# A spectral filter finished on VectorE with one inverse matmul per class: swapped rows by DMA instead of a second matmul

## The chip, the cores and the metric

The kernel runs on one core of a Trainium2 chip. The metric is the device time of one execution in microseconds (us); a comparison takes the median of several runs. The engines are TensorE (in the profile PE for matmuls and PEld for weight loads), VectorE (DVE), ScalarE (ACT), GpSimd (POOL) and SyncE (SP). The last two do little more here than issue DMA transfers: GpSimd the inputs and the output, SyncE the trips of intermediate results through DRAM.

## The reference

Two parts follow each other. A filter over the sequence (3008 positions, 8 batches, 256 channels) multiplies the real Fourier transform of x by a complex filter; then every token goes through a small network with a sine.

```python
X = np.fft.rfft(x, axis=1)                     # x: (8, 3008, 256)
Y = X * (filt_r + 1j * filt_i)[None, :, :]     # 1505 frequencies
y = np.fft.irfft(Y, n=3008, axis=1)
h = y.reshape(24064, 256) @ w_in               # w_in: (256, 2048)
s = np.sin(alpha * h)
out = (h + s * s / (alpha + 1e-09)) @ w_out    # w_out: (2048, 256)
```

## The kernel before

The transform of length 3008 = 47 x 64 is done as two short ones with twiddles folded into the second table. For each batch there are three stages of small pieces, with a trip through DRAM (a store and a transposed read) between them:

- stage 1, 8 pieces: transform of length 47 (`pa`), result `t1`, stored to `d1`, read back as `t2`;
- stage 2: transform of length 64 for two of the 24 classes a piece (`pb`, rows 0 to 63 the real and 64 to 127 the imaginary parts), product with the filter, inverse transform of length 64 (`pc`), result `g`, stored to `d2`;
- stage 3, 16 pieces: the inverse transform of length 47 (`pd`) from the reload `t4`, result `y`.

```python
def stage2(u):
    if u < 12:
        ps = (ops if b == 0 else fps).tile([128, 2, C], FP32, ...)          # pb
        for i in range(2):
            s = 2 * u + i
            nc.tensor.matmul(out=ps[:, i, :], lhsT=d_t[:, s, :], rhs=st["t2"][s // 6][:, s % 6, :], ...)
        xf = xfpool.tile([128, 2, C], FP16, ...)
        nc.scalar.copy(out=xf, in_=ps)
        pr = []
        for k in range(2):                            # times Re(F), times Im(F)
            pt = ppool.tile([128, 2, C], FP16, ...)
            nc.vector.tensor_tensor(out=pt, in0=xf, in1=f_t[k][:, 2 * u:2 * u + 2, :], op=ALU.mult)
            pr.append(pt)
        st["p", u] = pr
    if u > 0:
        w = u - 1
        pr = st.pop(("p", w))
        ...
        ps = fps.tile([128, 2, C], FP32, ...)                               # pc
        for i in range(2):
            for k in range(2):                        # two inverse tables, summed in PSUM
                nc.tensor.matmul(out=ps[:, i, :], lhsT=e_t[:, k, 2 * w + i, :], rhs=pr[k][:, i, :],
                                 start=(k == 0), stop=(k == 1))
        evac(st["g"][:, i0:i0 + 2, :], ps, ...)       # ScalarE or VectorE in turn
        if w % 3 == 2:
            ...                                       # two stores of g to d2, on SyncE
```

The second table `e_t[:, 1]` is the first one with its halves exchanged and one negated: it does the part of the complex product that mixes real and imaginary rows.

The network works on blocks of 512 tokens, eight steps a block. A step has four matmuls of 512 columns (`ph`, `hidden`), a sine on ScalarE and a square on VectorE, and nine matmuls of 256 columns for the block before (`po`, `project`). The pieces of the next batches are put between the steps by a plan, in which batch b's tokens begin at step 48b:

```python
plan = {1: [-45 + i for i in range(8)],
        2: [-29 + 14 * i / 13 for i in range(13)],
        3: [-10, -9] + [-7 + 2 * i for i in range(14)]}
...
at_step = 48 * b + plan[stage][at[stage]]
if b == 1 and stage == 1:
    at_step = 9 + at[stage]
```

Batch 0 has nothing to run beside. Its stages come first, and the load of `w_out` is told to wait for its first reload `t4`. A scheduler then orders the instructions of each engine, so a piece may stand a step or two behind the plan.

Of the kernel before, what the change touches and what calls it, by code (L numbers as in the profile page):

```python
# [9 lines left out]
FP16 = mybir.dt.float16  # L10
FP32 = mybir.dt.float32
# [43 lines left out]
def kernel(  # L55
# [33 lines left out]
    xpool = pool("xp", 4)  # L89
    t1pool = pool("t1", 4)  # L90
    t2pool = pool("t2", 4)
    xfpool = pool("xf", 3)
    ppool = pool("pp", 4)
    gpool = pool("gp", 4)
    t4pool = pool("t4", 3)
# [8 lines left out]
    wf_t = cpool.tile([NR, NK], FP16)  # L104
    nc.sync.dma_start(out=wf_t, in_=wf_dram.ap())
    d_t = cpool.tile([128, NS, 128], FP16)
    e_t = cpool.tile([128, 2, NS, 128], FP16)
    wi_t = cpool.tile([NK, NR], FP16)
    f_t = [cpool.tile([128, NS, C], FP16, name=f"filt{i}") for i in range(2)]

# [27 lines left out]
    def spectral(b):  # L138

        pieces = []  # L140
        d1 = dpool.tile([2 * NS, N2, C], FP16, name=f"d1_{b}", tag="d1")
        d2 = dpool.tile([2 * NS, N2, C], FP16, name=f"d2_{b}", tag="d2")
        d1_rows = d1.rearrange("a (h n) c -> (a h) n c", h=2)
        d2_rows = d2.rearrange("a (h n) c -> (a h) n c", h=2)
        st = {}

        def stage1(u):
            ch, half = divmod(u, 2)
            if u == 0:
                st["x"] = load_x(b)  # L150
            if half == 0:
                st["t1"] = t1pool.tile([NK, 8, C], FP16, name=f"t1_{b}_{ch}", tag="t1")
            for i in range(2):
                n0 = 4 * half + 2 * i
                ps = fps.tile([128, 512], FP32, name=f"pa_{b}_{u}_{i}", tag="f")
                marks["pe"] = nc.tensor.matmul(out=ps[0:NK, :], lhsT=wf_t, rhs=st["x"][ch][:, n0:n0 + 2, :],  # L156
                                               start=True, stop=True)
                evac(st["t1"][:, n0:n0 + 2, :], ps[0:NK, :])
            if half == 1:
                nc.sync.dma_start(out=d1_rows[:, 8 * ch:8 * ch + 8, :], in_=st["t1"])  # L160
            if u == 7:
                st["t2"] = []
                for g in range(4):
                    t2 = t2pool.tile([128, 6, C], FP16, name=f"t2_{b}_{g}", tag="t2")
                    for p in range(2):
                        a0 = p * NS + 6 * g
                        eng = nc.scalar if b == 0 and p else nc.sync
                        marks["t2", g] = eng.dma_start(out=t2[64 * p:64 * p + 64, :, :],
                                          in_=d1[a0:a0 + 6, :, :].rearrange("s n c -> n s c"))
                    st["t2"].append(t2)  # L170

        def stage2(u):
            if u < 12:

                ps = (ops if b == 0 else fps).tile([128, 2, C], FP32, name=f"pb_{b}_{u}",
                                                   tag="o" if b == 0 else "f")
                for i in range(2):
                    s = 2 * u + i
                    nc.tensor.matmul(out=ps[:, i, :], lhsT=d_t[:, s, :],  # L179
                                     rhs=st["t2"][s // 6][:, s % 6, :], start=True, stop=True)  # L180
                xf = xfpool.tile([128, 2, C], FP16, name=f"xf_{b}_{u}", tag="xf")
                nc.scalar.copy(out=xf, in_=ps)
                pr = []
                for k in range(2):
                    pt = ppool.tile([128, 2, C], FP16, name=f"p_{b}_{u}_{k}", tag="p")
                    marks["prod", u] = nc.vector.tensor_tensor(out=pt, in0=xf, in1=f_t[k][:, 2 * u:2 * u + 2, :],
                                                               op=ALU.mult)
                    pr.append(pt)
                st["p", u] = pr
            if u > 0:  # L190
                w = u - 1
                pr = st.pop(("p", w))
                if w % 3 == 0:
                    st["g"] = gpool.tile([128, 6, C], FP16, name=f"g_{b}_{w}", tag="g")
                ps = fps.tile([128, 2, C], FP32, name=f"pc_{b}_{w}", tag="f")
                for i in range(2):
                    for k in range(2):
                        nc.tensor.matmul(out=ps[:, i, :], lhsT=e_t[:, k, 2 * w + i, :],  # L198
                                         rhs=pr[k][:, i, :], start=(k == 0), stop=(k == 1))
                i0 = 2 * (w % 3)  # L200
                evac(st["g"][:, i0:i0 + 2, :], ps, i0 != 2 if b == 0 else None)
                if w % 3 == 2:
                    for p in range(2):
                        a0 = p * NS + 6 * (w // 3)
                        nc.sync.dma_start(out=d2[a0:a0 + 6, :, :].rearrange("s n c -> n s c"),
                                          in_=st["g"][64 * p:64 * p + 64, :, :])

        def stage3(u):
            ch, rest = divmod(u, 4)
            half, cb = divmod(rest, 2)  # L210
            if rest == 0:
                t4 = t4pool.tile([NK, 8, C], FP16, name=f"t4_{b}_{ch}", tag="t4")
                marks["t4"] = nc.sync.dma_start(out=t4, in_=d2_rows[:, 8 * ch:8 * ch + 8, :])
                st["t4"] = t4
            ps = fps.tile([128, 4, 128], FP32, name=f"pd_{b}_{u}", tag="f")
            psv = ps.rearrange("p a b -> p (a b)")[:, 0:4 * NR].rearrange("p (a r) -> p a r", r=NR)
            for i in range(4):
                nc.tensor.matmul(out=psv[:, i, :],
                                 lhsT=st["t4"][:, 4 * half + i, cb * 128:cb * 128 + 128],
                                 rhs=wi_t, start=True, stop=True)  # L220
            n0 = 8 * ch + 4 * half
            evac(y[:, cb, b % 2, n0:n0 + 4, :], psv)

        for u in range(8):
            pieces.append((1, lambda u=u: stage1(u)))
        for u in range(13):
            pieces.append((2, lambda u=u: stage2(u)))
        for u in range(16):
            pieces.append((3, lambda u=u: stage3(u)))
        return pieces  # L230
# [10 lines left out]
    first = spectral(0)  # L241
    for _, piece in first[:8]:
        piece()

# [19 lines left out]
    def dup_filter(g):  # L264
        gs = slice(6 * g, 6 * g + 6)
        for k in range(2):
            ins = nc.vector.tensor_copy(out=f_t[k][64:128, gs, :], in_=f_t[k][0:64, gs, :])
            behind(ins, marks["prod", 3 * g - 2] if g else s1_dve)

    for g in range(4):  # L270
        for k, filt in enumerate((filt_r, filt_i)):
# [8 lines left out]
    for g in range(3):  # L280
        pse = ops.tile([128, 8, 128], FP16, name=f"pse_{g}", tag="o")
        for i in range(8):
            behind(nc.tensor.transpose(out=pse[:, i, :], in_=d_t[:, 8 * g + i, :], identity=id16),
                   s1_pe)
        gs = slice(8 * g, 8 * g + 8)
        behind(nc.scalar.mul(e_t[:, 0, gs, :], pse, 0.125), s1_act)
        nc.vector.tensor_copy(out=e_t[0:64, 1, gs, :], in_=e_t[64:128, 0, gs, :])
        nc.vector.tensor_scalar(out=e_t[64:128, 1, gs, :], in0=e_t[0:64, 0, gs, :],
                                scalar1=-1.0, scalar2=None, op0=ALU.mult)

    ones = cpool.tile([128, 128], FP32)
    nc.vector.memset(ones, 1.0)
# [24 lines left out]
    w1T = cpool.tile([128, 16, C], FP16)  # L317
# [16 lines left out]
    def weights_out(i):  # L334
# [6 lines left out]
        if i < 4:  # L341
            pst = ops.tile([128, 8, 128], FP16, name=f"pst_{i}", tag="o")
            for cb in range(2):
                for t in range(4):
# [4 lines left out]
            for cb in range(2):  # L349
                nc.scalar.copy(out=w1T[:, 4 * i:4 * i + 4, cb * 128:cb * 128 + 128],  # L350
                               in_=pst[:, 4 * cb:4 * cb + 4, :])
        elif i >= 6:
            cb = i - 6
            psm = ops.tile([128, 2, C], FP32, name=f"psm_{cb}", tag="o")
            for jb in range(16):
                behind(nc.tensor.matmul(out=psm[:, 0, :], lhsT=w1T[:, jb, cb * 128:cb * 128 + 128],
                                        rhs=w2[:, jb, :], start=(jb == 0), stop=(jb == 15)),
                       marks["hidden"])
            nc.vector.tensor_copy(out=m_t[:, cb, :], in_=psm[:, 0, :])
# [44 lines left out]
    def store(o_blk, pb, col):  # L404

        p = 0
        while p < 128:
# [9 lines left out]

    plan = {1: [-45 + i for i in range(8)],
            2: [-29 + 14 * i / 13 for i in range(13)],
            3: [-10, -9] + [-7 + 2 * i for i in range(14)]}
    pending = [(1 + i % 4 + 8 * (i // 4), 0, piece) for i, (_, piece) in enumerate(first[25:])]
    for b in range(1, B):
        at = {1: 0, 2: 0, 3: 0}
        for stage, piece in spectral(b):
            at_step = 48 * b + plan[stage][at[stage]]
            if b == 1 and stage == 1:
                at_step = 9 + at[stage]  # L430
            at[stage] += 1
            pending.append((at_step, b, piece))
    pending.sort(key=lambda p: p[0])
    step = 0
# [44 lines left out]
```

## Time and profile before

| | before |
|---|---|
| median of 3 runs | 883.02 us (882.61 to 884.25) |
| span of the profiled run | 881.2 us |
| DMA moved | 94.99 MB, mean 108 GB/s |
| SyncE queue (hardware_dynamic q1) | 57008 packets, 50.36 MB, 22.0% of 16 engines |
| GpSimd queue (software_dynamic q0) | 23728 packets, 42.77 MB, 21.7% |
| HBM read, written | 58.02 MB, 49.81 MB |

Where the profile names a group, L198 are the inverse matmuls `pc`, L179 the forward ones `pb`, L186 the products on VectorE, L380 the squares, L375 and L390 the matmuls of the network. Tile numbers such as `t_2_0_2060` belong to one allocation; the first number is the batch. L160 stores `d1`, L168 reads `t2`, L205 stores `d2`, L213 reads `t4`. A timeline line has the start, the duration, engine, line, operation, tiles and how many instructions it merges; for a DMA the duration is that of its issue and not of the transfer. What an engine waited for stands in square brackets.

### The profile page before, as it was taken

The page shows a single profiled execution, that of the slowest core. Times are in us where ns is not written, and L with a number is a line of the kernel's source. Part 1 is how long each engine was busy: PE and PEld are TensorE (multiplying, and loading weights), DVE is VectorE, ACT ScalarE, POOL GpSimd, SP SyncE. Part 2 cuts the span into 40 slices and gives each one's busy share as a digit, 9 for nine tenths or more (in the row PEclk, how much of TensorE's full clock was granted, in tenths as well). Part 3 has the DMA queues.
Part 4 walks back from the last instruction along what each step waited for, and adds up shares of the span by engine and source line. Part 5 has one row for each costly group of instructions (what it writes and reads, how often), then busy time and mean ns, then how long its engine had stood idle before and what let it go on. Part 6 is the DMA issues. An engine that isn't in the chain of part 4 may idle for free.

```text
span 881.2 us, 15647 instructions
## 1 busy us (share of the span) xinstructions
PE 839.1 (95%) x6233; PEld 585.2 (66%) x6233; DVE 503.9 (57%) x886; ACT 521.1 (59%) x671; POOL 255.3 (29%) x495
## 2 busy tenths in 40 slices
PE   6759899999999999999999999999999999999993
PEld 2336677667776677767776677767776677667673
DVE  4737575566646565465756566565755666455441
ACT  4545565566656665666656666566656666555550
POOL 3211223333233232332233323233232232333332
PEclk9969999999999999999999999999999999999997
DMA  9984834185334724175343823256242533311111
GB/s 217 246 236 87 194 79 108 51 171 119 84 110 114 156 69 117 54 152 123 79 123 91 179 71 99 75 131 150 68 115 67 134 77 79 108 37 33 36 42 32
DMA packets 82737, 94.99 MB, mean 108 GB/s; under 512 B 12700, under 2 KB 64932, under 8 KB 82664
## 3 DMA queue, kind: packets, MB, share of 16 engines
q1 hardware_dynamic: 57008, 50.36, 22.0%
q0 software_dynamic: 23728, 42.77, 21.7%
q10 hardware_dynamic: 1928, 0.86, 0.5%
q8 instruction: 49, 0.80, 0.4%
q14 instruction: 24, 0.20, 0.1%
HBM read 58.02 MB, written 49.81 MB: 122 GB/s over the span
## 4 chain that ended last, share of the span: by engine, by line
PE 89%; DMA 6%; DVE 2%; issue 1%; ACT 0%; POOL 0%; SPq 0%; POOLq 0%; DVEq 0%
DMA w_out_502<-in_moe_w_out_dram 1%; DMA t_1_0_939<-d_1_504 1%; DMA d_7_517<-g_9_8756 1%; DMA d_0_107<-t_0_3_159 1%; DMA x_0_109<-in_x_dram 1%; DMA t_7_0_8931<-d_7_517 1%; DMA t_0_1_176<-d_0_107 0%; DMA t_0_0_476<-d_0_108 0%; PE po_0_5494 L390 0%; PE po_0_7950 L390 0%; PE po_2_4348 L390 0%; PE po_2_838 L390 0%; PE po_2_1892 L390 0%; PE po_0_705 L390 0%; PE po_0_4463 L390 0%
## 5 line engine op out<-in xcount | busy, mean ns | idle before, releaser
L375 PEld LDWEIGHTS <-w_465 128*128 128x128 f16 x1536 | 150.3, 98 | 100.4 <-issue 2.3
L198 PEld LDWEIGHTS <-e_t 128*128 128x128 f16 x384 | 37.5, 99 | 12.8 <-issue 2.5
L394 PEld LDWEIGHTS <-y 128*128 128x128 f16 x376 | 36.7, 98 | 4.7
L179 PEld LDWEIGHTS <-d_t 128*128 128x128 f16 x192 | 18.7, 100 | 27.6 <-DMA t_0_0_173<-d_0_107 3.5
L156 PEld LDWEIGHTS <-wf_t 94*96 94x96 f16 x128 | 16.5, 129 | 18.8 <-issue 9.4
L380 DVE TENSOR_TENSOR v_9644<-v_9644 128x1024 f16<-128x1024 f16 x8 | 5.5, 693 | 8.0 <-ACT v_9644 L379 8.0
L380 DVE TENSOR_TENSOR v_9789<-v_9789 128x1024 f16<-128x1024 f16 x8 | 5.5, 693 | 8.0 <-ACT v_9789 L379 8.0
L380 DVE TENSOR_TENSOR v_9488<-v_9488 128x1024 f16<-128x1024 f16 x8 | 5.5, 693 | 7.7 <-ACT v_9488 L379 7.7
L380 DVE TENSOR_TENSOR v_3898<-v_3898 128x1024 f16<-128x1024 f16 x8 | 5.5, 691 | 7.1 <-ACT v_3898 L379 7.1
L380 DVE TENSOR_TENSOR v_8810<-v_8810 128x1024 f16<-128x1024 f16 x8 | 5.5, 690 | 7.1 <-ACT v_8810 L379 7.1
L380 DVE TENSOR_TENSOR v_2681<-v_2681 128x1024 f16<-128x1024 f16 x8 | 5.5, 690 | 7.1 <-ACT v_2681 L379 7.1
L380 DVE TENSOR_TENSOR v_7593<-v_7593 128x1024 f16<-128x1024 f16 x8 | 5.5, 690 | 7.1 <-ACT v_7593 L379 7.1
L380 DVE TENSOR_TENSOR v_6354<-v_6354 128x1024 f16<-128x1024 f16 x8 | 5.5, 690 | 7.1 <-ACT v_6354 L379 7.1
L380 DVE TENSOR_TENSOR v_1442<-v_1442 128x1024 f16<-128x1024 f16 x8 | 5.5, 690 | 7.1 <-ACT v_1442 L379 7.1
L380 DVE TENSOR_TENSOR v_5137<-v_5137 128x1024 f16<-128x1024 f16 x8 | 5.5, 690 | 7.1 <-ACT v_5137 L379 7.1
L380 DVE TENSOR_TENSOR v_1608<-v_1608 128x1024 f16<-128x1024 f16 x8 | 5.5, 693 | 7.1 <-ACT v_1608 L379 7.1
L380 DVE TENSOR_TENSOR v_6520<-v_6520 128x1024 f16<-128x1024 f16 x8 | 5.5, 693 | 7.1 <-ACT v_6520 L379 7.1
L380 DVE TENSOR_TENSOR v_8976<-v_8976 128x1024 f16<-128x1024 f16 x8 | 5.5, 692 | 7.1 <-ACT v_8976 L379 7.1
L380 DVE TENSOR_TENSOR v_9147<-v_9147 128x1024 f16<-128x1024 f16 x8 | 5.5, 692 | 7.1 <-ACT v_9147 L379 7.1
L380 DVE TENSOR_TENSOR v_9317<-v_9317 128x1024 f16<-128x1024 f16 x8 | 5.5, 692 | 7.1 <-ACT v_9317 L379 7.1
L380 DVE TENSOR_TENSOR v_4064<-v_4064 128x1024 f16<-128x1024 f16 x8 | 5.5, 692 | 7.1 <-ACT v_4064 L379 7.1
L274 POOL DMA_DIRECT2D filt_101<-in_filt_r_dram x8 | 4.6, 587 | 16.9 <-DMA t_0_0_173<-d_0_107 15.0
(2527 smaller groups left out, 2688.4 us busy)
## 6 DMA issues: line engine op xcount, KB each, us to landing
w_in_469<-in_moe_w_in_dram POOLq DMA_DIRECT2D x2, 1024.0 KB, 9.2
w_out_502<-in_moe_w_out_dram POOLq DMA_DIRECT2D x1, 2048.0 KB, 12.3
filt_101<-in_filt_r_dram POOLq DMA_DIRECT2D x8, 96.0 KB, 7.0
filt_102<-in_filt_i_dram POOLq DMA_DIRECT2D x8, 96.0 KB, 7.4
d_t<-d_tbl SPq DMA_DIRECT2D x1, 768.0 KB, 7.9
d_0_107<-t_0_0_117 SPq DMA_DIRECT2D x1, 384.0 KB
d_0_107<-t_0_1_131 SPq DMA_DIRECT2D x1, 384.0 KB, 6.5
d_0_107<-t_0_2_145 SPq DMA_DIRECT2D x1, 384.0 KB
```

Source lines behind the costliest of these rows:

```text
L156: marks["pe"] = nc.tensor.matmul(out=ps[0:NK, :], lhsT=wf_t, rhs=st["x"][ch][:, n0:n0 + 2, :], start=True, stop=True)
L179: nc.tensor.matmul(out=ps[:, i, :], lhsT=d_t[:, s, :], rhs=st["t2"][s // 6][:, s % 6, :], start=True, stop=True)
L198: nc.tensor.matmul(out=ps[:, i, :], lhsT=e_t[:, k, 2 * w + i, :], rhs=pr[k][:, i, :], start=(k == 0), stop=(k == 1))
L274: ins = nc.gpsimd.dma_start(out=f_t[k][32 * q:32 * q + 32, 6 * g:6 * g + 6, :], in_=bass.AP(tensor=filt.tensor, offset=filt.offset + off, ...
L375: marks["hidden"] = nc.tensor.matmul(out=ps[:, i, 0:n], lhsT=w1[:, cb, jb * 128:jb * 128 + 128], rhs=y_cols[:, cb, c0:c0 + n], start=(cb = ...
L380: marks["square"] = nc.vector.tensor_tensor(out=vs, in0=vs, in1=vs, op=ALU.mult)
L394: nc.tensor.matmul(out=dst, lhsT=y_cols[:, cb, c0 + 128 * t:c0 + 128 * t + 128], rhs=m_t[:, cb, :], start=False, stop=(cb == 1))
```

## The change

The mixing part of the complex product moves from a second inverse matmul to VectorE. A copy `xs` of the spectrum with real and imaginary rows exchanged is made; VectorE forms xf times Re(F), xs times plus or minus Im(F), and their sum, and one inverse matmul per class follows. For batch 0 the exchanged spectrum is computed by TensorE itself (four half-width matmuls a piece and one more copy on ScalarE). For the other batches two DMAs on the SyncE queue copy it from SBUF to SBUF, for groups of three pieces, and the inverse comes five pieces behind the forward transform instead of one. The filter's imaginary part gets its sign by a negation of half its rows. To make room, `w1T` takes its space from the pool of `g`. The plan of pieces differs too: the diff replaces the one above.

```diff
-    xfpool = pool("xf", 3)
+    xfpool = pool("xf", 6)
...
-    e_t = cpool.tile([128, 2, NS, 128], FP16)
+    e_t = cpool.tile([128, NS, 128], FP16)
...
+        def forward(u):
+            ...                                   # tiles xf and xs for three pieces
+            nc.scalar.copy(out=xf[:, i0:i0 + 2, :], in_=ps)
+            if b == 0:
+                ps = ops.tile([128, 2, C], FP32, name=f"pw_{b}_{u}", tag="o")
+                for i in range(2):
+                    s = 2 * u + i
+                    for h in range(2):
+                        nc.tensor.matmul(out=ps[64 * h:64 * h + 64, i, :],
+                                         lhsT=d_t[:, s, 64 - 64 * h:128 - 64 * h],
+                                         rhs=st["t2"][s // 6][:, s % 6, :], start=True, stop=True)
+                nc.scalar.copy(out=xs[:, i0:i0 + 2, :], in_=ps)
+            elif u % 3 == 2:
+                for h in range(2):
+                    nc.sync.dma_start(out=xs[64 * h:64 * h + 64], in_=xf[64 - 64 * h:128 - 64 * h])
+
+        def inverse(w):
+            i0 = 2 * (w % 3)
+            pr = []
+            for k, name in enumerate(("xf", "xs")):
+                pr.append(ppool.tile([128, 2, C], FP16, name=f"p_{b}_{w}_{k}", tag="p"))
+                marks["prod", w] = nc.vector.tensor_tensor(
+                    out=pr[k], in0=st[name, w // 3][:, i0:i0 + 2, :],
+                    in1=f_t[k][:, 2 * w:2 * w + 2, :], op=ALU.mult)
+            nc.vector.tensor_tensor(out=pr[0], in0=pr[0], in1=pr[1], op=ALU.add)
+            ...
+            for i in range(2):
+                nc.tensor.matmul(out=ps[:, i, :], lhsT=e_t[:, 2 * w + i, :], rhs=pr[0][:, i, :],
+                                 start=True, stop=True)
+            evac(st["g"][:, i0:i0 + 2, :], ps)
+            ...                                   # stores to d2 as before
+
+        lag = 1 if b == 0 else 5
...
+            if k == 1:
+                nc.vector.tensor_scalar(out=f_t[1][0:64, gs, :], in0=f_t[1][0:64, gs, :],
+                                        scalar1=-1.0, scalar2=None, op0=ALU.mult)
...
-        behind(nc.scalar.mul(e_t[:, 0, gs, :], pse, 0.125), s1_act)
-        nc.vector.tensor_copy(out=e_t[0:64, 1, gs, :], in_=e_t[64:128, 0, gs, :])
-        nc.vector.tensor_scalar(out=e_t[64:128, 1, gs, :], in0=e_t[0:64, 0, gs, :],
-                                scalar1=-1.0, scalar2=None, op0=ALU.mult)
+        behind(nc.scalar.mul(e_t[:, gs, :], pse, 0.125), s1_act)
...
-    plan = {1: [-45 + i for i in range(8)],
-            2: [-29 + 14 * i / 13 for i in range(13)],
-            3: [-10, -9] + [-7 + 2 * i for i in range(14)]}
+    starts = {1: -36, 2: -23, 3: -5}
+    steps = {1: 8, 2: 16, 3: 16}
+    count = {1: 8, 2: 17, 3: 16}
...
-            at_step = 48 * b + plan[stage][at[stage]]
+            i = at[stage]
+            at[stage] += 1
+            at_step = 48 * b - 8 + starts[stage] + i * steps[stage] / count[stage]
             if b == 1 and stage == 1:
-                at_step = 9 + at[stage]
+                at_step = 9 + i
```

More of the change, by code (lines that the diff above doesn't have):

```diff
@@ L170, in stage1 @@
                     st["t2"].append(t2)
+        def forward(u):
+            if u % 3 == 0:
+                for name in ("xf", "xs"):
+                    st[name, u // 3] = xfpool.tile([128, 6, C], FP16, name=f"{name}_{b}_{u}",
+                                                   tag="xf")
+            i0 = 2 * (u % 3)
+            xf, xs = st["xf", u // 3], st["xs", u // 3]
+            ps = (ops if b == 0 else fps).tile([128, 2, C], FP32, name=f"pb_{b}_{u}",
+                                               tag="o" if b == 0 else "f")
+            for i in range(2):
+                s = 2 * u + i
+                nc.tensor.matmul(out=ps[:, i, :], lhsT=d_t[:, s, :],
+                                 rhs=st["t2"][s // 6][:, s % 6, :], start=True, stop=True)
[3 more added lines that the diff above has]
+                for i in range(2):
+                    s = 2 * u + i
+                    for h in range(2):
+                        nc.tensor.matmul(out=ps[64 * h:64 * h + 64, i, :],
+                                         lhsT=d_t[:, s, 64 - 64 * h:128 - 64 * h],
+                                         rhs=st["t2"][s // 6][:, s % 6, :], start=True, stop=True)
+                nc.scalar.copy(out=xs[:, i0:i0 + 2, :], in_=ps)
+            elif u % 3 == 2:
+                for h in range(2):
+                    nc.sync.dma_start(out=xs[64 * h:64 * h + 64], in_=xf[64 - 64 * h:128 - 64 * h])
@@ new lines, in inverse @@
+        def inverse(w):
[7 more added lines that the diff above has]
+            nc.vector.tensor_tensor(out=pr[0], in0=pr[0], in1=pr[1], op=ALU.add)
+            if w % 3 == 0:
+                st["g"] = gpool.tile([128, 6, C], FP16, name=f"g_{b}_{w}", tag="g")
+            ps = fps.tile([128, 2, C], FP32, name=f"pc_{b}_{w}", tag="f")
+            for i in range(2):
+                nc.tensor.matmul(out=ps[:, i, :], lhsT=e_t[:, 2 * w + i, :], rhs=pr[0][:, i, :],
+                                 start=True, stop=True)
+            evac(st["g"][:, i0:i0 + 2, :], ps)
+            if w % 3 == 2:
+                for p in range(2):
+                    a0 = p * NS + 6 * (w // 3)
+                    nc.sync.dma_start(out=d2[a0:a0 + 6, :, :].rearrange("s n c -> n s c"),
+                                      in_=st["g"][64 * p:64 * p + 64, :, :])
@@ L172, in stage2 @@
+        lag = 1 if b == 0 else 5
         def stage2(u):
             if u < 12:
[L175 to L206, printed above, removed]
@@ L208, in stage3 @@
+                forward(u)
+            if u >= lag:
+                inverse(u - lag)
         def stage3(u):
@@ L225, in spectral @@
             pieces.append((1, lambda u=u: stage1(u)))
-        for u in range(13):
+        for u in range(12 + lag):
             pieces.append((2, lambda u=u: stage2(u)))
@@ L267, in dup_filter @@
             ins = nc.vector.tensor_copy(out=f_t[k][64:128, gs, :], in_=f_t[k][0:64, gs, :])
-            behind(ins, marks["prod", 3 * g - 2] if g else s1_dve)
+            behind(ins, marks["prod", 3 * g - 3] if g else s1_dve)
+            if k == 1:
+                nc.vector.tensor_scalar(out=f_t[1][0:64, gs, :], in0=f_t[1][0:64, gs, :],
+                                        scalar1=-1.0, scalar2=None, op0=ALU.mult)
     for g in range(4):
@@ L316 @@
     m_t = cpool.tile([128, 2, C], FP16)
-    w1T = cpool.tile([128, 16, C], FP16)
+    w1T = [gpool.tile([128, 6, C], FP16, name=f"w1T_{i}", tag="g") for i in range(3)]
     w_in32 = vpool.tile([128, 2, DFF], FP32, name="w_in32", tag="v")
@@ L348, in weights_out @@
                                                identity=id16), marks["hidden"])
-            for cb in range(2):
-                nc.scalar.copy(out=w1T[:, 4 * i:4 * i + 4, cb * 128:cb * 128 + 128],
-                               in_=pst[:, 4 * cb:4 * cb + 4, :])
+            for h in range(2):
+                j0 = 4 * i + 2 * h
+                nc.scalar.copy(
+                    out=w1T[j0 // 6][:, j0 % 6:j0 % 6 + 2, :].rearrange("p j (a c) -> p a j c", a=2),
+                    in_=pst.rearrange("p (a j) c -> p a j c", a=2)[:, :, 2 * h:2 * h + 2, :])
         elif i >= 6:
@@ L355, in weights_out @@
             for jb in range(16):
-                behind(nc.tensor.matmul(out=psm[:, 0, :], lhsT=w1T[:, jb, cb * 128:cb * 128 + 128],
+                behind(nc.tensor.matmul(out=psm[:, 0, :], lhsT=w1T[jb // 6][:, jb % 6, cb * 128:cb * 128 + 128],
                                         rhs=w2[:, jb, :], start=(jb == 0), stop=(jb == 15)),
@@ L427 @@
         for stage, piece in spectral(b):
-            at_step = 48 * b + plan[stage][at[stage]]
+            i = at[stage]
+            at[stage] += 1
+            at_step = 48 * b - 8 + starts[stage] + i * steps[stage] / count[stage]
             if b == 1 and stage == 1:
-                at_step = 9 + at[stage]
-            at[stage] += 1
+                at_step = 9 + i
             pending.append((at_step, b, piece))
```

## The prediction

> **What bounds the kernel now.** I read the busy shares first, then the busy time by stretches, then the chain that ended last. The page begins:
>
> ```profile
> span 881.2 us, 15647 instructions
> PE 839.1 (95%) x6233; PEld 585.2 (66%) x6233; DVE 503.9 (57%) x886; ACT 521.1 (59%) x671; POOL 255.3 (29%) x495
> ```
>
> PE looks full, but matmul ends overlap, so I checked stretches (columns: window, length, then busy us of PE, PEld, DVE, ACT, POOL with counts, granted clock, DMA share, GB/s):
>
> ```profile
> 27.00:44.00 17.00, 13.00 (x72) 7.25 (x70) 15.51 (x36) 11.00 (x20) 6.09 (x10) 0.92 1.10 272
> 44.00:51.50 7.50, 0.00 (x0) 0.00 (x0) 3.23 (x3) 0.00 (x0) 0.00 (x0) 0.50 0.72 192
> 245.00:490.00 245.00, 245.00 (x1862) 173.09 (x1861) 146.43 (x253) 153.71 (x199) 75.30 (x146) 1.00 0.46 111
> ```
>
> Two regimes. From about 105 us on PE never idles: I took the start-to-start times of consecutive matmuls, and they are the streaming times, 216 ns for 512 columns, 109 for 256, 41 for 94, with no gap. There a removed matmul is saved time. At 27 to 44 us (middle stage of batch 0) VectorE is the full engine, 15.5 of 17 us; then PE waits 7.5 us for a round trip through DRAM.
>
> The later batches need two such trips each, both hidden by the distance between pieces. Batch 2, first trip: its last stage-1 matmul ends at 188.2 and the transposed read `t2` goes out when the stores have landed:
>
> ```profile
> 189.32 0.30 SPq L160 DMA_DIRECT2D d_2_506<-t_2_3_2030  x1
> 197.29 1.28 SPq L168 DMA_DIRECT2D t_2_0_2060<-d_2_506  x2
> ```
>
> It lands at 201.5 (3.5 us after the second issue) and is used at 205.5: 13.3 us needed, 17.3 available. Second trip: the last inverse matmul ends at 237.7, then
>
> ```profile
> 238.52 1.25 SPq L205 DMA_DIRECT2D d_2_507<-g_9_2627  x2
> 243.78 0.31 SPq L213 DMA_DIRECT2D t_2_0_2801<-d_2_507  x1
> ```
>
> By the DMA records this read lands at 246.8 and is used at 248.6: 9.1 needed, 10.9 available. In batch 7 that trip already shows as a stall:
>
> ```profile
> 753.99 0.34 PE L218 MATMUL pd_0_8933<-wi_t,t_7_0_8931 96*128 96x94 f16 x4 [0.29 <-DMA t_7_0_8931<-d_7_517]
> ```
>
> **What the Trainium skill says.** "TensorE: Matmul & The Clock Gate", section "Back-to-back issue gap", gives N/2.4 + 2.5 ns for a warm matmul, 109 ns at 256 columns; the trace agrees (109). "DMA: Bandwidth & Descriptors", section "Anatomy of one DMA", puts about 2 us of fixed cost on a DMA, mostly the receipt of the write. The quietest stores here take 2.9 us to land, so a swap by DMA costs latency, hardly bandwidth. "VectorE: DVE Perf Modes", section "The perf-mode tier table", caps a tensor_tensor at 2x, while a plain copy from SBUF may go 4x: the added sum will cost as much as a product. The trace has 418 ns for a 128x512 product, 335 ns from start to start when packed.
>
> **The change part by part.**
>
> 1. Inverse matmuls: 24 of 256 columns fewer per batch. Batches 1 to 7: 7 x 24 x 109 ns = 18.3 us, all on the path. Gain 18.3.
>
> 2. Batch 0 fits the VectorE-bound stage. Before, its stage is 24 products (8.0 us), 6 copies of the filter (3.1), 4 evacuations (2.4) = 13.6 us. After, by the built program's order: 36 products and sums x 0.335 = 12.1, 6 copies 3.1, 3 negations at about 0.43 = 1.3, 6 evacuations x 0.608 = 3.6, and some 0.8 for sums that wait for their own product = 20.9 us. The last evacuation is on VectorE too, just behind its matmul. Net about 6.3 us later. PE gets 48 half-width matmuls, ScalarE 12 more copies (30 x 0.48 = 14.4 us); both stay below VectorE. What follows (store, reload, the 12.3 us load of w_out that waits for this reload) is serial, so the 6.3 us go through to the end. Loss 6.3.
>
> 3. The schedule, which the short description does not name, is the largest item. Stage 1 now runs at steps 48b-44 to -37 and stage 2 starts at -31; before, -45 to -38 and -29: two or three steps less of distance. Stage 2 is longer (17 pieces at lag 5) and ends at -15; stage 3 starts at -13 instead of -10. I counted the matmuls in the built order of the new program and gave each its streaming time. A plain step (4 x 216 + 9 x 109 ns) is 1.85 us.
> First trip: 10.9 us available (17.3 before). Needed, from before, in batches 2 to 6: 13.3, 12.7, 12.8, 12.7, 12.8; in batch 7, with no x of a next batch loading beside it, 9.9. Stalls 2.4 + 1.8 + 1.9 + 1.8 + 1.9 + 0 = 9.8; the x loads stand in the same places, so I keep 9.4 after rounding down for noise. Batch 1 keeps its distance and its present 3.4 us stall.
> Second trip: 7.6 us available (10.9 before), as the order holds stage 3 back to about 4 steps behind the last inverse. Needed: 8.6 to 10.5 in the seven batches (issue of the reload 5.5 to 6.9 us after the last inverse, plus about 3.1 of reload). Stalls 1.0 to 2.9. The stores should be a little less disturbed, as the neighbouring output stores move by a step: 1.3 each, 9. Loss 18.4 together.
>
> 4. The swap. Per group of three pieces: two DMAs of 192 KB on the SyncE queue. From the last forward matmul: ScalarE's copy ends 1.3 us later (behind a 1.02 us sine), issue 0.65, landing about 2.9 like the quiet stores, then a product, a neighbour's product and the sum, 1.2: about 6.2 us with semaphores. The order leaves 6.4, 6.7, 7.6 and 6.3. Hidden, but barely; I allow 0.4 us a batch.
>
> 5. VectorE in stage 2. In twelve steps it now has 36 products and sums (12.1), 12 squares x 0.609 (7.3), 6 evacuations (3.6), 3 output copies (2.0) and 1.2 of own waits: 26.2 us; PE has 7 x 2.28 + 5 x 2.07 = 26.3. That is full, and it runs in order, with PE waiting for its sums and its evacuations. I allow 0.6 us a batch. Parts 4 and 5: 7.
>
> Sum: 883 - 18.3 + 6.3 + 18.4 + 7 = 896; I say 895.
>
> **The rivals.** (a) Plain PE saving: if the trips and the swap stay hidden and start-up does not move, 883 - 18 = 865. For it: 140 us and 245 us stretches with PE at 100%. Against: the distances in 3 are below what the trace shows as needed in six and seven batches. (b) VectorE takes over: if swap and sums stall each group of three by 1 us, 28 groups add 28 instead of 7, about 916. For it: 26.2 against 26.3 us. Against: squares have slack of more than a step, and idle time outside stage 2 is ample (57% busy overall). (c) Start-up hides its 6 us, because the DMA for w_out or the filters ends it anyway: 889. Against: w_out is issued only behind the reload. (d) The trips get shorter since stage 1 no longer runs beside stage 3 of the batch before: half the stalls vanish, 886.
>
> **Range and chances.** The saving is certain to 1 us; start-up to 3, the trips to 6, swap and VectorE to 8, combined about 10 to 11: 880 to 910 for 8 in 10. Faster by 2% needs under 865.4, which is rival (a) whole: 0.05. Slower by 2% needs over 900.7, five above the centre: 0.28. Within: 0.67.
>
> **What would show it.** PE has 6233 matmuls less 192 plus 48 = about 6089. PE waits of 1.5 to 2.5 us on the `t2` read at the head of stage 2 in batches 2 to 6 and not in 7, and of 1 to 3 us on the `t4` read at the head of stage 3 in every batch. The first reload of batch 0 is issued at about 54 us instead of 47.6. VectorE's busy time rises by 96 x 0.42 = 40 us, to about 540. Waits for `xs` on VectorE are short. If the two trips do not show on PE, part 3 fails and the time is near 878; if PE waits for sums in most groups, rival (b) holds.

## The result and the profile after

| | before | after |
|---|---|---|
| median | 882.82 us (882.27 to 884.25, 4 runs) | 894.67 us (892.17 to 896.36, 4 runs) |
| ratio | | 1.0129, 95% interval 1.0099 to 1.016 |
| span of the profiled run | 881.2 us | 894.1 us |
| SyncE queue | 57008 packets, 50.36 MB, 22.0% | 61488 packets, 61.38 MB, 26.0% |

The change costs 12 us, which is within 2%. The page of the changed kernel begins:

```profile
span 894.1 us, 15435 instructions
PE 834.7 (93%) x6089; PEld 565.5 (63%) x6089; DVE 531.3 (59%) x982; ACT 529.1 (59%) x681; POOL 254.9 (29%) x495
```

The count of matmuls is the predicted 6089. VectorE is busy 27 us more, not 40: packed operations of 0.42 us start 0.335 us apart, and busy time counts their overlap once. Products and sums count 33.8 us more, the squares 4.4 less, as more of them now overlap with a neighbour. The stretches, with the columns of before:

```profile
27.00:44.00 17.00, 15.06 (x85) 6.23 (x86) 14.00 (x32) 14.20 (x26) 5.65 (x10) 1.00 1.01 243
44.00:52.00 8.00, 3.34 (x12) 0.76 (x12) 7.20 (x20) 2.27 (x5) 0.00 (x0) 0.58 0.42 95
52.00:61.00 9.00, 0.76 (x8) 0.68 (x9) 5.17 (x5) 0.23 (x1) 0.25 (x1) 0.50 0.60 153
245.00:490.00 245.00, 238.72 (x1818) 165.74 (x1816) 151.24 (x279) 151.16 (x194) 72.74 (x141) 1.00 0.48 118
```

Two things are to be seen. Batch 0's middle stage now fills the stretch up to 52 us, and the hole that follows it (the trip through DRAM) lies there instead of at 44 us. And in the long steady stretch PE, which never paused before, is idle for 6.3 of 245 us.

The two trips of batch 2 by the timeline: first the last store of stage 1, the transposed read and the matmul that waits for it, then the store of stage 2, the reload and its matmul.

```profile
203.39 0.30 SPq L160 DMA_DIRECT2D d_2_562<-t_2_3_2126  x1
209.62 1.28 SPq L168 DMA_DIRECT2D t_2_0_2156<-d_2_562  x2
213.92 0.39 PE L184 MATMUL pb_0_2283<-t_2_0_2156,d_t 128*128 128x256 f16 x2 [0.57 <-DMA t_2_0_2156<-d_2_562]
...
251.04 1.25 SPq L220 DMA_DIRECT2D d_2_563<-g_9_2688  x2
254.79 0.31 SPq L236 DMA_DIRECT2D t_2_0_2786<-d_2_563  x1
258.34 0.34 PE L241 MATMUL pd_0_2788<-wi_t,t_2_0_2786 96*128 96x94 f16 x4 [0.38 <-DMA t_2_0_2786<-d_2_563]
```

Both reads, which used to land before they were wanted, are now waited for. Batch 0's reload and its first use show the later start; the first two lines are from before:

```profile
47.62 0.32 SPq L213 DMA_DIRECT2D t_0_0_476<-d_0_108  x1
51.51 0.49 PE L218 MATMUL pd_0_478<-wi_t,t_0_0_476 96*128 96x94 f16 x4 [8.68 <-DMA t_0_0_476<-d_0_108]
...
56.46 0.32 SPq L236 DMA_DIRECT2D t_0_0_532<-d_0_108  x1
...
60.24 0.49 PE L241 MATMUL pd_0_534<-wi_t,t_0_0_532 96*128 96x94 f16 x4 [8.33 <-DMA t_0_0_532<-d_0_108]
```

For the whole run I took the start-to-start time of consecutive matmuls, subtracted the streaming time of the first, and booked the rest on the matmul that came late. From the first stage-3 matmul of batch 0 on:

| PE time lost ahead of, us | before | after | after by batch 1 to 7 |
|---|---|---|---|
| first `pb` of batches 1 to 7 (first trip) | 3.3 | 8.7 | 3.3, 0.7, 1.9, 1.0, 1.8, 0, 0 |
| first `pd` of batches 1 to 7 (second trip) | 0.5 | 6.7 | 1.2, 0.6, 1.2, 0.8, 0.8, 1.3, 0.8 |
| `pc` of batches 1 to 7 (sum on VectorE) | 1.4 | 10.9 | 2.2, 1.2, 2.4, 1.4, 1.3, 1.2, 1.2 |
| everything else | 10.8 | 12.1 | |
| sum | 16.0 | 38.4 | |

The balance closes: 22.4 us more lost here, 8.7 us later in starting, 18.3 us of matmuls less, together 12.8; the spans differ by 12.9.

### The profile page after: what moved, and what is told of

The parts are those of the page before. It is cut to its first block, busy times and chain, and to the rows that moved or that the text cites. A ratio compares the mean times of both kernels' runs of the same rounds, so it can differ in the third digit from the quotient of the medians.

```text
span 894.1 us, 15435 instructions
## 1 busy us (share of the span) xinstructions
PE 834.7 (93%) x6089; PEld 565.5 (63%) x6089; DVE 531.3 (59%) x982; ACT 529.1 (59%) x681; POOL 254.9 (29%) x495
## 3 DMA queue, kind: packets, MB, share of 16 engines
q1 hardware_dynamic: 61488, 61.38, 26.0%
## 4 chain that ended last, share of the span: by engine, by line
PE 71%; DMA 16%; DVE 5%; ACT 3%; issue 2%; SPq 1%; POOL 0%; DVEq 0%; POOLq 0%; ACTq 0%
DMA w_out_558<-in_moe_w_out_dram 1%; DMA d_3_564<-t_3_3_3336 1%; DMA d_4_566<-t_4_3_4566 1%; DMA d_2_562<-t_2_3_2126 1%; DMA t_1_0_995<-d_1_560 1%; SPq L220 1%; DMA t_5_0_5806<-d_5_568 1%; DMA d_5_568<-t_5_3_5776 1%; DMA d_0_107<-t_0_3_159 1%; DMA x_0_109<-in_x_dram 1%; DMA xs_9_3739<-xf_9_3738 1%; DMA xs_9_1299<-xf_9_1298 1%; DMA t_0_0_173<-d_0_107 0%; DMA t_3_0_3995<-d_3_565 0%; ACT v_980 L405 0%
## 5 line engine op out<-in xcount | busy, mean ns | idle before, releaser
L214 PEld LDWEIGHTS <-e_t 128*128 128x128 f16 x192 | 14.1, 99 | 28.8 <-issue 3.8
## 6 DMA issues: line engine op xcount, KB each, us to landing
w_out_558<-in_moe_w_out_dram POOLq DMA_DIRECT2D x1, 2048.0 KB, 12.6
```

The costliest lines, as they stand in the source:

```text
L214: nc.tensor.matmul(out=ps[:, i, :], lhsT=e_t[:, 2 * w + i, :], rhs=pr[0][:, i, :], start=True, stop=True)
```

## The experiments

Each run stands beside runs of the kernel before on the same chip, so the ratios are what compares across sets; one ratio point of 0.01 is 8.8 us. The changed kernel was run again in the second set (f1), at 1.0131.

| run | edit | median us | ratio to before, 95% |
|---|---|---|---|
| e1 | changed kernel, wider plan | 888.93 | 1.0047 (1.0029 to 1.0065) |
| e2 | changed kernel, batch 0 in the old form | 893.16 | 1.0097 (1.0076 to 1.0119) |
| e3 | both | 880.58 | 0.9964 (0.9953 to 0.9975) |
| e4 | kernel before with the new plan | 888.78 | 1.0049 (1.0032 to 1.0066) |
| f1 | changed kernel again | 896.17 | 1.0131 (1.0103 to 1.0159) |
| f2 | changed kernel without the exchange | 886.12 | 1.0024 (1.0010 to 1.0038) |
| f3 | changed kernel without the sum | 891.36 | 1.0080 (1.0051 to 1.0110) |
| f4 | e3 with more distance | 875.11 | 0.9890 (0.9865 to 0.9915) |
| g1 | changed kernel with lag 6 | 894.94 | 1.0119 (1.0089 to 1.0150) |
| g2 | e2 again | 894.35 | 1.0116 (1.0088 to 1.0144) |
| g3 | f4 with lag 6 | 867.80 | 0.9818 (0.9793 to 0.9843) |

### Is it the plan? (e1, e4)

e1 moves only step numbers, for batches 2 to 7:

```diff
-            at_step = 48 * b - 8 + starts[stage] + i * steps[stage] / count[stage]
+            first_step = {1: -49, 2: -34, 3: -13}[stage] if b > 1 else starts[stage] - 8
+            at_step = 48 * b + first_step + i * steps[stage] / count[stage]
```

> The changed kernel with one thing altered: stage 1 of batches 2 to 7 starts at step 48b-49 instead of 48b-44 and stage 2 at 48b-34 instead of 48b-31; stage 3, batch 0 and batch 1 stay. By the built order the first trip then has 14.8 us of matmuls to hide behind (11.1 before) and the second 9.0 (7.7). Theory (the plan's short distances cost PE 5.3 us at the head of stage 2 and 5.5 us at the head of stage 3 in batches 2 to 7): those waits vanish and the time falls by 9 to 11 us, to about 884 to 886. Rival (VectorE, full in stage 2, is the bound and the waits only move to its sums): the time stays within 3 us of 894.7 and the waits of the inverse matmuls grow.

e4 gives the kernel before the step numbers of the changed one, and nothing else of the change:

```diff
...
-            at_step = 48 * b + plan[stage][at[stage]]
...
+            at_step = 48 * b + {1: -44, 2: -31, 3: -13}[stage] + i * {1: 1, 2: 16 / 17, 3: 1}[stage]
```

> The kernel before with the step numbers of the changed plan (13 pieces in stage 2, so that its end stays as far from stage 3 as before: 11.1 us; the first trip has 11.1 us instead of 17.4). Theory (a trip of 11 to 13 us does not fit into 11 us, whatever the inverse looks like): waits of 0 to 2 us at the head of stage 2 in batches 2 to 6, 5 us in all, 887 to 889. Rival (the waits come from the extra traffic of the swap): no such waits, 883.

e1 gained 7.3 us by the ratios (1.0130 to 1.0047), against 9 to 11 expected: the first trip's waits in batches 2 to 7 went whole (5.4 us), the second trip's fell from 6.7 to 3.8, the waits ahead of `pc` stayed (11.6), and 2.3 us were given back ahead of stage-1 matmuls, which now overlap stage 3 of the batch before. e4 lost 5.1 us, as the theory said. Its trace has the first trip's wait in a kernel that has no exchange and no sum; this is batch 3:

```profile
305.64 0.39 PE L179 MATMUL pb<-t,d_t 128*128 128x256 f16 x2 [1.39 <-DMA t<-d]
```

Its account has 0.5, 1.6, 0.8, 1.6, 0.5 and 0 us for batches 2 to 7, 5.0 in all; the second trip, which has 11.1 us of room there, shows nothing. So the first trip's share comes from the step numbers alone. The traffic of the exchange is not the main part of it: f2 below, which has no exchange in batches 1 to 7, still loses 7.9 us on the first trip and 8.4 on the second, against 9.8 and 8.7 in f1. What is left for the second trip is the short distance of the changed order, 7.7 us, which e1 widened to 9.0.

### Is it the start? (e2, g2, e3, f1)

Batch 0 goes back to two inverse tables, two products and no sum, without the half-width matmuls; the negation of the filter moves behind its stage 2:

```diff
-            for k, name in enumerate(("xf", "xs")):
+            for k, name in enumerate(("xf", "xf" if b == 0 else "xs")):
...
-            nc.vector.tensor_tensor(out=pr[0], in0=pr[0], in1=pr[1], op=ALU.add)
+            if b > 0:
+                nc.vector.tensor_tensor(out=pr[0], in0=pr[0], in1=pr[1], op=ALU.add)
...
+                if b == 0:
+                    nc.tensor.matmul(out=ps[:, i, :], lhsT=e2_t[:, 2 * w + i, :], rhs=pr[1][:, i, :],
+                                     start=False, stop=True)
```

> The changed kernel with batch 0 done as in the kernel before: two inverse tables and two products without a sum, no half-width matmuls, and the negation of the filter moved behind batch 0's stage 2. Theory (batch 0's stage 2 is bound by VectorE and everything behind it is serial): the first stage-3 matmul comes back from 60.2 to about 51.5 us and the whole time falls by 8 to 9 us, to about 886. Rival (the load of w_out or another transfer ends the start in any case): the first stage-3 matmul comes earlier, but the time falls by less than 3 us.

> The two alterations together: wider plan and batch 0 in the old way. If they act on separate stretches of PE, as the theory says, the gains add: 18 to 20 us off 894.7, about 875 to 877, and so some 6 to 8 us below the kernel before (what the inverse matmuls saved, 18.3 us, less about 10 us of waits for sums). If one hides the other, 884 to 886.

> The changed kernel once more, so that it stands beside the other runs of this set. It has been measured only four times (892.2 to 896.4 us). If batch 0 in the old form really saves only about 1.5 us, this median lies at 893.5 to 895.5, and the 7 us of earlier start were given back in longer trips. If that small saving was chance in the few runs, this median lies at 896 or above.

> Batch 0 in the old form once more. It began stage 3 of batch 0 7.8 us earlier, but was only 3 us faster than the changed kernel by the ratios to the kernel before (1.0097 against 1.0131 and 1.0129). If 4 us are given back for good in the tight schedule, the ratio is 1.008 to 1.011 again. If that was chance of the transfers in those runs, the ratio falls to 1.003 to 1.006, as the pair with the wider plan (880.6 against 888.9) says.

f1 came out at 896.17 us, where its text calls the small saving chance; but the kernel before was slower in that set too, and by the ratio (1.0131) nothing had changed. g2, at 1.0116, lies just above the 1.008 to 1.011 that stand for a saving given back for good.

In e3 the edit is worth 8.3 us against e1 by the medians of the same set, 7.3 by the ratios: the whole of the later start, as stage 3 of batch 0 begins 8.0 us earlier than in e1. The hole of batch 0 ends where it did before (51.51):

```profile
51.81 0.81 PE L246 MATMUL pd<-wi_t,t 96*128 96x94 f16 x8 [8.73 <-DMA t<-d]
```

e3 missed its 875 to 877 by 3.6 us or more, for the 12.3 us ahead of `pc` and 3.4 us of second trips stayed. In the tight plan the same edit is worth only 2.1 us (mean ratio of e2 and g2 1.0107, of the two sets of the changed kernel 1.0130). My expectation for e2 was wrong, and the repeat showed that it was no chance. The profiles of both pairs say where it went: stage 3 of batch 0 starts 7.4 us earlier (53.0 and 53.2 against 60.2 and 60.8), and from there 44.7 us are lost instead of 39.7: 3.4 more ahead of `pc`, 2.4 more on the second trip, 0.6 less on the first. The part on `pc` can be followed in the traces. In the changed kernel's batch 2 the exchange lands in 3.0 us beside four output stores (DMA view of 219 to 224 us: size, median us to landing):

```profile
xs_0_2282<-xf_0_2281 SPq DMA_DIRECT2D x2, 192.0 KB, 3.0
out_dram<-o_1_2338 POOLq DMA_DIRECT2D x1, 82.0 KB, 2.8
```

In e2 the same transfers with the same neighbours (210.5 to 216.5 us) take a microsecond longer, and the queue list has one more entry, a fetch of instructions:

```profile
q8 instruction: 1, 0.02, 1.0%
...
xs<-xf SPq DMA_DIRECT2D x2, 192.0 KB, 4.3
out_dram<-o POOLq DMA_DIRECT2D x1, 82.0 KB, 4.0
```

and the first inverse matmul of that batch waits:

```profile
217.39 0.39 PE L214 MATMUL pc<-p,e_t 128*128 128x256 f16 x2 [0.89 <-DVE p L209]
```

In e2 a fetch starts during 8 of the 28 exchanges, in the changed kernel during 3, and the five largest waits ahead of `pc` in e2 (0.65 to 1.08 us) all follow such an exchange. The section on the hardware below has the count over all runs. Why 2.4 us more went to the second trip is open; the two profiles of the changed kernel differ there by 2 us themselves.

### What makes PE wait for the sum? (f2, f3, g1)

f2 leaves out the exchange in batches 1 to 7 (both products read xf, so the mixing part is missing); f3 leaves out the sum there (the inverse reads the first product only).

```diff
-            elif u % 3 == 2:
-                for h in range(2):
-                    nc.sync.dma_start(out=xs[64 * h:64 * h + 64], in_=xf[64 - 64 * h:128 - 64 * h])
...
-            for k, name in enumerate(("xf", "xs")):
+            for k, name in enumerate(("xf", "xs" if b == 0 else "xf")):
```

```diff
-            nc.vector.tensor_tensor(out=pr[0], in0=pr[0], in1=pr[1], op=ALU.add)
+            if b == 0:
+                nc.vector.tensor_tensor(out=pr[0], in0=pr[0], in1=pr[1], op=ALU.add)
```

> In batches 1 to 7 the exchange of real and imaginary rows is left out: both products read xf, no exchange DMA is issued; the number of VectorE instructions is unchanged. Theory (the waits ahead of the inverse matmuls, 10.9 us in all, come from VectorE being full): 891 to 894 us, the waits of 0.4 us ahead of the first inverse matmul of each batch stay. Rival (they come from the exchange landing late): the waits go to 2 us or less and the time to 886 or below.

> In batches 1 to 7 VectorE does not add the two products (84 instructions of 0.335 us fewer); the inverse matmul reads the first product only; the exchange stays. Theory (VectorE full): the waits ahead of the inverse matmuls fall from 10.9 us to about 3, and the time to 886 to 889 us. Rival (the exchange lands late): the waits stay above 8 us and the time within 2 us of the changed kernel, 892 or above.

Both took the waits ahead of `pc` away whole: 10.4 us in f1, 0.2 in f2, 0.6 in f3. f2 is 10 us faster than f1; f3 is 5, as 3 us came back on the two trips. f2 met what the rival foretold (2 us or less and 886 or below; 0.2 and 886.1): VectorE at its full count of instructions does not make PE wait when nothing has to land first. f3, at 891.4, met neither of its two forecasts, and it shows less than I meant it to. Its inverse reads only the product of xf, which is made before the exchange lands, so f3 takes the exchange off the path to the first inverse as well as the sum off VectorE. Batch 4 in f3: the product that the first inverse reads, the first product with xs, and that inverse, which does not wait:

```profile
417.18 0.42 DVE L206 TENSOR_TENSOR p<-xf,filt 128x512 f16<-128x512 f16 x1
...
425.59 0.42 DVE L206 TENSOR_TENSOR p<-xs,filt 128x512 f16<-128x512 f16 x1
...
426.01 0.38 PE L215 MATMUL pc<-p,e_t 128*128 128x256 f16 x2
```

So the exchange is needed for the waits; how much it costs without the sum behind it is not shown by these two runs. How it joins VectorE's work is seen in the order there. The changed kernel, batch 4, on both sides of the exchange's landing (its second DMA is issued at 425.3 and lands 3.0 us later):

```profile
424.24 0.69 DVE L406 TENSOR_TENSOR v_4696<-v_4696 128x1024 f16<-128x1024 f16 x1 [1.37 <-ACT v_4696 L405]
...
428.37 0.69 DVE L406 TENSOR_TENSOR v_4696<-v_4696 128x1024 f16<-128x1024 f16 x1 [1.37 <-ACT v_4696 L405]
428.98 0.42 DVE L206 TENSOR_TENSOR p_0_1_4842<-xs_0_4722,filt_102 128x512 f16<-128x512 f16 x1
429.31 0.42 DVE L206 TENSOR_TENSOR p_1_0_4872<-xf_0_4721,filt_101 128x512 f16<-128x512 f16 x1
429.65 0.42 DVE L209 TENSOR_TENSOR p_0_0_4840<-p_0_0_4840,p_0_1_4842 128x512 f16<-128x512 f16 x1
429.98 0.42 DVE L206 TENSOR_TENSOR p_1_1_4874<-xs_0_4722,filt_102 128x512 f16<-128x512 f16 x1
430.32 0.42 DVE L206 TENSOR_TENSOR p_2_0_4909<-xf_0_4721,filt_101 128x512 f16<-128x512 f16 x1
430.65 0.69 DVE L406 TENSOR_TENSOR v_4696<-v_4696 128x1024 f16<-128x1024 f16 x1
```

The matmul that this sum feeds:

```profile
430.12 0.39 PE L214 MATMUL pc_0_4846<-p_0_0_4840,e_t 128*128 128x256 f16 x2 [0.24 <-DVE p_0_0_4840 L209]
```

Before the landing VectorE is idle between squares (1.37 us at a time); after it, three pieces' work comes at once, each operation behind the last, and in order with the squares. One square stands ahead of the first product, 0.61 us, and the sum ends 1.7 us after the landing. In f2 the products need no exchange and are spread over the steps before; the wait in the second line is for a matmul to be done with the product's buffer:

```profile
422.21 0.69 DVE L403 TENSOR_TENSOR v<-v 128x1024 f16<-128x1024 f16 x1 [0.77 <-ACT v L402]
423.66 0.42 DVE L203 TENSOR_TENSOR p<-xf,filt 128x512 f16<-128x512 f16 x1 [0.75 <-PE pc L211]
424.12 0.42 DVE L206 TENSOR_TENSOR p<-p,p 128x512 f16<-128x512 f16 x1
```

From the first to the last inverse of batch 4, VectorE is busy for 22.55 of 24.9 us in the changed kernel and for 21.69 of 24.0 in f2, the same nine tenths; PE loses time only in the changed kernel. The first line is the changed kernel's:

```profile
430.10:455.00 24.90, 24.76 (x177) 16.73 (x178) 22.55 (x51) 17.10 (x25) 6.89 (x14) 1.00 0.48 122
```

```profile
423.20:447.20 24.00, 24.00 (x179) 17.36 (x178) 21.69 (x45) 17.51 (x24) 6.42 (x13) 1.00 0.31 75
```

g1 gives the exchange one piece more, in the same 16 steps:

```diff
-        lag = 1 if b == 0 else 5
+        lag = 1 if b == 0 else 6
...
-    count = {1: 8, 2: 17, 3: 16}
+    count = {1: 8, 2: 18, 3: 16}
```

> The changed kernel with the inverse six pieces behind the forward transform instead of five, and nothing else (the distances of the two trips in the built order stay 11.1 and 7.7 us; those of the exchange grow from 6.4 to 7.7 us to 7.6 to 8.5). Leaving out the exchange and leaving out the sum each took the waits ahead of the inverse matmuls away whole, so theory: they come from the short time between the landing of the exchange and the matmul, in which VectorE must do its share; one piece more takes 7 to 9 of the 10.4 us away, 887 to 890 us against the 896.2 of the changed kernel. Rival (VectorE is full over the stage as a whole, whatever the distance): at most 3 us, 893 or above.

This missed: 1.1 us by the ratio, and the waits ahead of `pc` fell from 10.4 only to 6.9. They had moved. The first piece of a batch no longer waits in batches 2 to 7 (0.4 us each before); some of the fourth to the ninth do, the fifth longest (0.33 us in each of these batches), where PE waits for an evacuation, the copy of a `g` out of PSUM, on VectorE. Batch 4:

```profile
440.21 0.38 PE L214 MATMUL pc<-p,e_t 128*128 128x256 f16 x2 [0.16 <-DVE g L136]
```

About 1 us more than in f1 went to the first trip. Eighteen pieces in the steps of seventeen make VectorE fuller still, 24.61 of 26 us (from the first inverse at 431.9 us to the last, 21.71 of 23.0):

```profile
429.00:455.00 26.00, 25.80 (x185) 17.67 (x184) 24.61 (x55) 17.85 (x25) 6.65 (x13) 1.00 0.47 118
```

### A version that beats both (f4, g3)

f4 is e3 with stage 2 over 20 steps and stage 3 later; g3 adds lag 6, with 21 steps and one more step of head start. The step numbers of g3:

```diff
...
-            at_step = 48 * b - 8 + starts[stage] + i * steps[stage] / count[stage]
+            if b == 1:
+                first_step, over = {1: (-44, 8), 2: (-29.5, 15.5), 3: (-10, 16)}[stage]
+            else:
+                first_step, over = {1: (-50, 8), 2: (-35 if b % 2 else -34, 21),
+                                    3: (-10 if b % 2 else -6, 16)}[stage]
+            at_step = 48 * b + first_step + i * over / count[stage]
             if b == 1 and stage == 1:
-                at_step = 9 + i
+                at_step = 7 + i
```

> The changed kernel with batch 0 in the old form and a plan with more distance everywhere: in batches 2 to 7 stage 1 starts at step 48b-49, stage 2 is spread over 20 steps instead of 16 (from 48b-34 or 48b-33), stage 3 starts at 48b-10 in odd and 48b-6 in even batches; batch 1 starts stage 1 two steps earlier. Streaming times in the built order give 14.4 or 16.6 us for the first trip and 9.2 or 14.1 for the second (7.7 in batch 1). Theory: the waits at the heads of stages 2 and 3 fall to about 3 us in all, those ahead of the inverse matmuls from 12.3 to about 8; 880.6 - 4 - 4 = 873 to 877 us, faster than the kernel before by 0.8 to 1.2%. Rival (more overlap of the stages only moves the waits): 879 or above.

> The best so far (batch 0 in the old form, wider plan) with lag six: stage 1 starts at step 48b-50, stage 2 at 48b-35 or 48b-34 over 21 steps; the first trip has 14.5 or 16.1 us, the second 9.2 or 14.1. Theory: the waits ahead of the inverse matmuls fall from 8.0 us to 2 or 3, the others stay: 875.1 - 5 = 869 to 872 us. Rival (the longer stage pushes other waits up by as much): 874 or above.

f4 came out as expected, and g3 1 us below its range: 867.8 us, 1.8% faster than before (interval 1.6 to 2.1%). With the runs above, the loss ahead of `pc` makes a small table:

| | 16 steps | 20 or 21 steps |
|---|---|---|
| lag 5 | 10.4 to 14.2 | 8.0 |
| lag 6 | 6.9 | 0.6 |

Only lag 6 with the longer stage takes all of it away. The columns differ in more than the room on VectorE, though: the matmuls between the last forward matmul of a group and its first inverse stream for 6.4 to 7.7 us in the changed kernel, 6.5 to 8.7 in f4, 7.6 to 8.5 in g1 and 8.3 to 10.8 in g3 (batches 2 to 7). So these runs do not part the time for the exchange from the room on VectorE; that VectorE has a share of its own is read from g1's wait for an evacuation. In g3 the trips lose 3.1 us in all, of which 2.8 are batch 1's, and the steady stretch is full again:

```profile
PE 822.7 (95%) x6065; PEld 568.4 (66%) x6065; DVE 532.3 (62%) x974; ACT 522.6 (60%) x671; POOL 255.3 (30%) x495
...
245.00:490.00 245.00, 244.78 (x1855) 171.10 (x1854) 158.13 (x283) 157.18 (x205) 75.82 (x147) 1.00 0.56 132
```

## Why the prediction was right, and where it was not

The total was right (895 predicted, 894.67 measured), and so was the reason: a sure saving on PE, given back at the start, on two trips and ahead of the sums. That the centre came within 0.4 us is luck: the schedule was taken 6.8 us too large, batch 0 and the sums together 4.9 too small, and 1.3 us more was lost elsewhere.

1. **Inverse matmuls, −18.3.** Right. The count is exact, the balance closes with it, and g3, which has almost none of the other costs, gains 16.3 us over before in medians (884.1 to 867.8), with a start 1.0 us later and 1.0 us more lost than before's profile.

2. **Batch 0, +6.3.** The mechanism held: the time goes through to the end, as e3 against e1 shows with 7 to 8 us. The size was off: 8.7 us. (The two sums there, 20.9 and 13.6, differ by 7.3; how 7.3 became 6.3 is not said.) The sum of 20.9 us took VectorE as the one full engine. The stage ran 24.35 us (28.29 to 52.64). VectorE was busy for 21.84 of them, 1.7 more than the sum has without its waits, and idle for 2.5 where I allowed 0.8: 1.95 us of this went in three waits for an inverse matmul, two of which are these:

```profile
38.01 0.69 DVE L136 CAST g_3_354<-pc_3_355 128x512 f16<-128x512 f32 x1 [0.97 <-PE pc_3_355 L214]
...
51.95 0.69 DVE L136 CAST g_9_484<-pc_11_513 128x512 f16<-128x512 f32 x1 [0.70 <-PE pc_11_513 L214]
```

The term that failed is this 0.8, which counted only VectorE's waits for its own products. From 27 to 44 us PE (15.06 of 17 us) and ScalarE (14.20) had become as full as VectorE (14.00); that the three wait for each other is read from these figures and not tried by an edit. The reload at 56.46 instead of "about 54" says the same.

3. **The schedule, +18.4.** The right cause (e4 shows the first trip's share by itself), too large: 5.4 us for the first trip where I had 9.4, 6.2 for the second where I had 9. I carried the needs over from before. For batches 2 to 7 they became 11.6, 12.7, 11.8, 12.6, 10.6 and 8.5, with waits of 0.7 to 1.9 us where I gave 1.5 to 2.5, and none in batch 6. Only batches 3 and 5 kept theirs. The second trip's reload went out 4.5 to 5.0 us after the last inverse, against 5.5 to 6.9, because the last pair of stores landed sooner. e4 has the same 4.5 to 4.6 us in every batch and much the same waits on the first trip, so the trips got shorter with the step numbers and not with the exchange. This is rival (d), "the trips get shorter", in part; which transfer no longer stands beside the stores was not tried.

4. **and 5. Exchange and VectorE, +7.** Measured 9.5 more than before (10.9 against 1.4). The exchange's latency was right: 3.0 us to landing in most groups, where I had 2.9. What the Trainium skill says there ("DMA: Bandwidth & Descriptors", "Anatomy of one DMA": a fixed cost of about 2 us) it says of transfers that GpSimd issues, and these go out on SyncE; here a quiet exchange takes 2.4 us from the second issue to its last packet and 3.0 to the landing. The sum costs as much as a product, 0.42 us in the lines above, as "VectorE: DVE Perf Modes", "The perf-mode tier table", led me to expect. The step that failed is the separation: "hidden, but barely" for the one and "that is full" for the other, added up. f2 shows that the full VectorE costs nothing without the exchange; what costs, by the lines of batch 4, is their series, a late landing and then three pieces' work in order on an engine that is nine tenths busy. There the path from the last forward matmul to the first inverse took 6.9 us where part 4 had 6.2 and the order leaves 6.4: part 4 has a product, a neighbour's product and the sum behind the landing, but not the square of 0.61 us that stands ahead of them. As the sign for it I had named waits on the exchange, and those are indeed short; the loss stood in the wait for the sum.

The rivals: (a) needed hidden trips and an unmoved start, and g3 is what that looks like (867.8, for the 865 given). (b) had the right place, at a third of its size per group. (c) fell with e3.

The range of 880 to 910 held with much room: the largest miss of a term was 7 us, that of the trips.

## What to carry to other kernels

When a change comes with new step numbers, measure for every trip how long it needs and how long the new order gives it: here step numbers, lag and the form of batch 0 decide between a loss of 12 us and a gain of 16. Two small slacks that lie in series are judged together: here the landing of the exchange and the VectorE work behind it, squares included. Before an experiment that leaves out one of the two is read, see whether it takes the other off the path as well, as f3 did. A stage that has nothing to run beside (batch 0) may keep the old form when the new one moves work onto the engine that bounds it.

## What the runs showed of the hardware

Exchanges during which an instruction fetch starts take longer. The profile's instruction queue q8 carries packets of 16 KB, 47 in the changed kernel's run, some 18 us apart, each taking 1.04 us in the median. In ten profiles with the exchange (280 exchanges of two times 192 KB), the time from the second issue to the end of the last packet is 2.4 us in the median for the 235 without a fetch starting meanwhile (18 of them over 3.4 us), and 3.6 us for the 45 with one (31 over 3.4). Their place in the program does not explain it: in the four profiles of the changed kernel's plan at lag 5 (the changed kernel, f1, e2, g2), 12 of the 28 exchanges meet a fetch in some runs and not in others, and in the mean of the runs all 12 take longer with one, by 0.9 us in the median; between the changed kernel and f1 alone, though, two differ so, and take the same time. No run moved a fetch on purpose, so the cause is read from this coincidence and not shown by an edit. It would explain why an edit in batch 0 alone changed the waits of batch 7 in both of its profiles: another instruction stream places the fetches elsewhere.
